# Batch 0's queries in two blocks, the first layer beginning on block one while block two is scored

## Chip, cores, metric

One core of one Trainium2 chip. The metric is the device time of a run in microseconds (us). Every time quoted is a median of runs unless said otherwise.

## The reference

Sigmoid attention over 8 batches of 12 heads, 448 positions and 64 columns a head; then an MLP with a tanh-approximated gelu on 3584 rows.

```python
scores = scale * np.matmul(q, k.transpose(0, 1, 3, 2)) - np.log(S)     # S = 448
attn = 1.0 / (1.0 + np.exp(-scores))
x = heads_side_by_side(np.matmul(attn, v))                             # 3584 x 768
h = x @ w_in                                                           # 768 x 2048
g = 0.5 * h * (1.0 + np.tanh(c * (h + 0.044715 * h * h * h)))
out = g @ w_out                                                        # 2048 x 768
```

## The kernel before

The kernel plans its own order. It holds a list of operations with dependencies and assumed costs, plays them through on paper, and emits each engine's instructions in the order found. Four heads make a group (3 groups a batch); a unit is a group's scores against 64 keys (7 units a group). "qk" is a score matmul, "av" a value matmul, "A" the first layer, "B" the second, "evx" the copy of an attention result into `xT`, the input of A. Heads are scored through the sigmoid function in batch 0, later through tanh and an affine step on the vector engine (DVE), since 1/(1+exp(-x)) is 0.5 tanh(x/2) + 0.5.

```python
units = [(g, j) for g in range(G) for j in range(NJ)]
EARLY = ("v0 q2 v1 v2 q3 v3 w0 w1 q4 v4 w2 q5 v5 w3 o0 o1 o2 o3").split()   # order of the early loads
# ... in make_qk, for unit n of group g: four 64x64 matmuls of 448 columns, then
if g < SIG * NG:                                  # batch 0: sigmoid, on the scalar engine (ACT)
    tanh[n] = aff[n] = plan.add(Op("sig%d" % n, "ACT",
        lambda e: e.activation(at[as_][:], both, AF.Sigmoid, bias=bias, scale=scale),
        [op, old], 2 * S / 1.2 + 60, 2 * S / 1.2 + 210, prio=(1, n)))
    if n == SIG * NG * NJ - 1:                    # after the last sigmoid: touch gelu's table once
        plan.add(Op("warm2", "ACT", lambda e: e.activation(warm[:], warm[:], AF.Gelu_apprx_tanh),
                    [tanh[n]], 1500.0, 1500.0))
else:                                             # later batches: tanh (ACT), then affine (DVE)
    ...
# ... in make_a: A of batch b, column block fc of the 2048, six 128x128 matmuls of 448 columns
deps = [prev] + [evac[(b, kt)] for kt in range(KT)]
# ...
ev = plan.add(Op("gelu%d.%d" % (b, fc), "ACT", ..., gdeps, S / 1.2 + 50, S / 1.2 + 190, prio=(0, b)))
```

The last two numbers of an operation are what the plan believes that it occupies and takes. No plan cost depends on the function computed before it. A has to wait for all three groups of its batch, so in batch 0 it waits for all 21 sigmoids.

Of the kernel before, what the change touches and what calls it, by code (L numbers as in the profile page):

```python
# [266 lines left out]
def bass_sigmoid_attention__then__act_gelu_tanh_kernel(  # L267
# [24 lines left out]
    NQT = 3  # L292
# [12 lines left out]
    with contextlib.ExitStack() as stack:  # L305
# [73 lines left out]


        G = B * NG
        units = [(g, j) for g in range(G) for j in range(NJ)]
        cast_q, cast_k, tr_q, tr_k, ld_q, ld_k, ld_v = {}, {}, {}, {}, {}, {}, {}
        freed_q, freed_k = {}, {}
        qk, tanh, aff, av, evac = {}, {}, {}, {}, {}
        trans = []

        EARLY = ("v0 q2 v1 v2 q3 v3 w0 w1 q4 v4 w2 q5 v5 w3 o0 o1 o2 o3").split()
# [19 lines left out]
        def load_qk(g):  # L408
            b, i = divmod(g, NG)
            s = g % NQF  # L410
            for (nm, src, dst, low, ld, cast, freed) in (("k", k, kf, kb, ld_k, cast_k, freed_k),
                                                         ("q", q, qf, qb, ld_q, cast_q, freed_q)):
                ap = flat4(src, b, i).rearrange("(c p x) -> p c x", c=2, p=128)
                if low_load(nm, g):
# [9 lines left out]
                                    + ([lambda: w_out_ld[3][0]] if PE_TR * NG <= g < PE_TR * NG + NG else []), 500.0, 0.0,  # L424
                                    prio=(2, g), sem="ld%s%d" % (nm, s), pkt=(16, 85.0)))
# [16 lines left out]
        def cast_qk(g):  # L442
            s = g % NQF
            for (nm, src, dst, ld, cast, freed) in (("k", kf, kb, ld_k, cast_k, freed_k),
                                                    ("q", qf, qb, ld_q, cast_q, freed_q)):
                if low_load(nm, g):
# [6 lines left out]
                                      [ld[g]] + later(freed, g - NQF), 660.0, 720.0, prio=(1, g), alts=alts))  # L453
# [16 lines left out]
        def trans_ready(t):  # L470
            if not trans or eye.end is None or eye.end > t or free_pairs(t) < 1:
                return False
            g, nm, src, dst, cast, tr, freed, after = trans[0]
            return g in cast and cast[g].end is not None and cast[g].end <= t
# [35 lines left out]
        def make_qk(n, t):  # L510
            g, j = units[n]
# [5 lines left out]
            both = ps[:, x:y + 1, 0:S]  # L517
            kv, qv = by_half(kT[s], g), by_half(qT[s], g)

            def fn(e):  # L520
                r = None
                for (a, c, half) in ((0, 0, 0), (0, 1, 1), (1, 1, 0), (1, 0, 1)):
                    d = slice(64 * c, 64 * c + 64)
                    r = mm(ps[64 * half:64 * half + 64, (x, y)[a], 0:S],  # L524
                           kv[d, a, j, :], qv[d, a, :, :],
# [3 lines left out]
            qk[(g, j)] = op = Op("qk%d.%d" % (g, j), "PE", fn, [tr_q[g], tr_k[g]] + prev,  # L529
                                 4 * 2.5 + S / 2.4, 165.0, mode=64)  # L530
            pg, pj = units[n - NAT] if n >= NAT else (None, None)
            old = av[pg] if pg is not None else None
            if g < SIG * NG:
                tanh[n] = aff[n] = plan.add(Op("sig%d" % n, "ACT",
                                               lambda e: e.activation(at[as_][:], both, AF.Sigmoid,  # L535
                                                                      bias=bias, scale=scale),
                                               [op, old], 2 * S / 1.2 + 60, 2 * S / 1.2 + 210, prio=(1, n)))
                if n == SIG * NG * NJ - 1:
                    plan.add(Op("warm2", "ACT", lambda e: e.activation(warm[:], warm[:], AF.Gelu_apprx_tanh),
                                [tanh[n]], 1500.0, 1500.0))  # L540
            else:
                tanh[n] = plan.add(Op("tanh%d" % n, "ACT",
                                      lambda e: e.activation(th[ts][:], both, AF.Tanh,  # L543
                                                             bias=0.5 * bias, scale=0.5 * scale),
                                      [op, aff.get(n - NTH)], 2 * S / 1.2 + 60, 2 * S / 1.2 + 210, prio=(1, n)))
                aff[n] = plan.add(Op("aff%d" % n, "DVE",
                                     lambda e: e.tensor_scalar(at[as_][:], th[ts][:], 0.5, 0.5,  # L547
                                                               op0=ALU.mult, op1=ALU.add),
                                     [tanh[n], old], 640.0, 710.0, prio=(2, n)))
# [6 lines left out]
        def make_av(g, t):  # L556
            b, i = divmod(g, NG)
# [4 lines left out]
            for j in range(NJ):  # L562
                n = g * NJ + j
                as_ = n % NAT

                def fn(e, j=j, as_=as_):
                    r = None
                    for (a, c, half) in ((0, 0, 0), (0, 1, 1), (1, 0, 1), (1, 1, 0)):
                        d = slice(64 * half, 64 * half + 64)
                        slot = half if a == 0 else 1 - half  # L570
                        r = mm(ps[64 * c:64 * c + 64, banks[a], 0:S],  # L571
                               vb[s][d, slot, j, :],
                               at[as_][d, a, :],
# [4 lines left out]
                ops.append(Op("av%d.%d" % (g, j), "PE", fn, deps, 4 * 2.5 + S / 2.4, 165.0, mode=64))  # L578
            av_open.append((g, banks, ops))
# [4 lines left out]
        def close_av():  # L584
            g, banks, ops = av_open.pop()
            b, i = divmod(g, NG)
            for j in range(NJ):
                ops[j].deps = [d for d in ops[j].deps + [aff[g * NJ + j]]]
            av[g] = ops[-1]
            xb = b % NXT  # L590
            for a in range(2):
                deps = [ops[-1]]
                if b >= NXT:
                    deps.append(a_last[b - NXT])
                op = plan.add(Op("evx%d.%d" % (g, a), "ANY",
                                 lambda e, who, a=a: copy(e, xT[xb][:, 2 * i + a, :], ps[:, banks[a], 0:S], who),
                                 deps, 0, 0, prio=(0, g),
                                 alts=copy_alts(S) if b else {"DVE": copy_alts(S)["DVE"]}))
# [351 lines left out]
```

## Time and profile before

| | before |
|---|---|
| time (first 3 runs) | 395.24 us |
| span | 393.7 us |
| tensor engine (PE) busy | 378.2 us, 96% |
| first sigmoid, last sigmoid's end | 9.74 us, 27.7 us |
| first A | 29.60 us |
| table loads on ACT | 2 |

The page's busy line, and two lines of its chain of waits:

```profile
PE 378.2 (96%) x3344; PEld 196.0 (50%) x3344; DVE 135.6 (34%) x227; ACT 240.7 (61%) x377; POOL 50.9 (13%) x82
...
PE 92%; ACT 4%; DMA 2%; DVE 0%; issue 0%; SPq 0%; ACTq 0%
```

Busy time says that PE is nearly full, but the matmuls are counted with their modelled ends. I kept a ledger. Its rates come from dense stretches of this trace: 12 matmuls of A (448 columns) take 2.27 us and 16 of B (384 columns) 2.60 us, which makes 2.4 columns per ns and 2.5 ns more for each matmul; 28 transposes take 0.25 us, and the four 64x64 matmuls of a unit count as one pass of their columns. The work so counted is the useful PE time, 356.6 us in all; what remains of the elapsed time is "excess". In the kernel before, excess reaches 19.0 us at 30 us and grows by 14.5 us in the next 320 us. So over half of it lies in the head, and there time is to be had. ACT around its only later table load, with start, duration and instruction:

```profile
26.62 1.09 ACT L535 ACTIVATE at<-ps 128x896 bf16<-128x896 f32 x1
27.42 1.10 ACT L543 ACTIVATE th<-ps 128x896 f32<-128x896 f32 x1
28.54 1.28 ACT L539 ACT_TABLE_LOAD   x1
29.83 0.20 ACT L539 ACTIVATE warm<-warm 128x1 f32<-128x1 f32 x1
```

Two neighbouring starts are 0.80 us apart, though each takes about 1 us: activations overlap. The load doesn't overlap anything. And PE in the same place (the bracket is idle time before it and what ended it):

```profile
26.95 0.38 PE L524 MATMUL ps<-qT,kT 64*64 64x448 bf16 x4 [0.24 <-ACT at L535]
27.16 0.36 PE L571 MATMUL ps<-at,vb 64*64 64x448 bf16 x4
27.76 0.38 PE L524 MATMUL ps<-qT,kT 64*64 64x448 bf16 x4 [0.24 <-ACT at L535]
...
29.60 2.44 PE L616 MATMUL ps<-xT,w_in 128*128 128x448 bf16 x12 [0.38 <-DVE xT L335]
```

In each 0.81 us PE has two units of work, which take 0.19 us each in dense stretches; the trace counts it busy for 0.57 us and idle for 0.24, waiting for a sigmoid.

### The profile page before, as it was taken

The numbers are of one execution on the slowest core, as the hardware profiler recorded it, in microseconds if no ns is written. First come the engines' busy times: TensorE is split into PE (matmuls) and PEld (weight loads), VectorE is DVE, ScalarE is ACT, GpSimd is POOL, SyncE is SP. The second block draws the span as 40 slices with busy tenths as digits, with TensorE's granted clock in tenths as the row PEclk, the third lists the DMA queues.
The fourth block names the chain that finished last, engine by engine and source line by source line (L and its number), as shares of the span: only waits on it lengthen the run. The fifth ranks groups of instructions, "written<-read, shape, count | busy, mean of one in ns | idle before, by whom it ended". The sixth has DMA issues, their size and how long they took to land.

```text
span 393.7 us, 7728 instructions
## 1 busy us (share of the span) xinstructions
PE 378.2 (96%) x3344; PEld 196.0 (50%) x3344; DVE 135.6 (34%) x227; ACT 240.7 (61%) x377; POOL 50.9 (13%) x82
## 2 busy tenths in 40 slices
PE   2879999999999999999999999999999999999996
PEld 1424545555544554554554555555454555555563
DVE  3426643136545515545444343343333210000000
ACT  1999973477779757777657666576647632333211
POOL 6992110011102010101110101101000000000000
PEclk9999999999999999999999999999999999999999
DMA  8999999728689466768767448727211011111133
GB/s 230 199 199 203 210 190 301 163 52 176 166 214 207 123 140 155 162 157 184 179 115 180 133 78 177 183 47 182 65 40 42 2 40 42 40 42 40 40 82 80
DMA packets 63490, 51.76 MB, mean 131 GB/s; under 512 B 36192, under 2 KB 60000, under 8 KB 63456
## 3 DMA queue, kind: packets, MB, share of 16 engines
q1 hardware_dynamic: 48848, 37.53, 37.8%
q0 software_dynamic: 14528, 13.64, 21.9%
q8 instruction: 26, 0.43, 0.4%
q10 hardware_dynamic: 80, 0.10, 0.1%
q14 instruction: 8, 0.07, 0.1%
HBM read 45.61 MB, written 11.01 MB: 144 GB/s over the span
## 4 chain that ended last, share of the span: by engine, by line
PE 92%; ACT 4%; DMA 2%; DVE 0%; issue 0%; SPq 0%; ACTq 0%
PE ps L616 37%; PE ps L653 37%; PE ps L524 9%; PE ps L571 8%; ACT at L535 3%; DMA kf<-in_k_dram 2%; ACT th L543 1%; PE ps L490 1%; DVE xT L335 0%; ACT gT L629 0%; SPq L422 0%; DVE kb L335 0%; ACT xT L334 0%; ACT ob L334 0%; ACTq L888 0%
## 5 line engine op out<-in xcount | busy, mean ns | idle before, releaser
L616 PE MATMUL ps<-xT,w_in 128*128 128x448 bf16 x768 | 155.5, 353 | 0.5 <-DVE xT L335 0.4
L653 PE MATMUL ps<-w_out,gT 128*128 128x384 bf16 x896 | 153.1, 326 | 0.0
L547 DVE TENSOR_SCALAR at<-th 128x896 bf16<-128x896 f32 x147 | 92.0, 626 | 139.0 <-ACT th L543 138.8
L543 ACT ACTIVATE th<-ps 128x896 f32<-128x896 f32 x147 | 129.1, 929 | 0.1
L653 PEld LDWEIGHTS ps<-w_out,gT 128*128 128x128 bf16 x896 | 86.3, 98 | 63.3 <-ACT th L543 2.9
L616 PEld LDWEIGHTS ps<-xT,w_in 128*128 128x128 bf16 x768 | 71.7, 98 | 76.7 <-ACT th L543 3.9
L629 ACT ACTIVATE gT<-ps 128x448 bf16<-128x448 f32 x128 | 71.2, 556 | 43.2 <-PE ps L616 43.1
L334 ACT ACTIVATE ob<-ps 128x384 f32<-128x384 f32 x56 | 27.5, 490 | 95.4 <-PE ps L653 95.4
L524 PE MATMUL ps<-qT,kT 64*64 64x448 bf16 x672 | 48.8, 368 | 4.0 <-ACT at L535 3.7
L436 POOL DMA_DIRECT2D vb<-in_v_dram x24 | 14.5, 604 | 216.8 <-PE ps L524 213.9
L571 PE MATMUL ps<-at,vb 64*64 64x448 bf16 x672 | 40.1, 356 | 0.2
L524 PEld LDWEIGHTS ps<-qT,kT 64*64 64x64 bf16 x672 | 15.0, 106 | 32.3 <-issue 14.4
L571 PEld LDWEIGHTS ps<-at,vb 64*64 64x64 bf16 x672 | 19.9, 109 | 11.8 <-issue 1.3
L535 ACT ACTIVATE at<-ps 128x896 bf16<-128x896 f32 x21 | 17.4, 971 | 8.0 <-PE ps L524 7.9
L335 DVE CAST xT<-ps 128x448 bf16<-128x448 f32 x27 | 16.4, 618 | 11.5 <-PE ps L571 11.5
L335 DVE CAST kb<-kf 128x896 bf16<-128x896 f32 x20 | 12.5, 624 | 18.1 <-DMA kf<-in_k_dram 17.8
L438 POOL DMA_DIRECT2D vb<-in_v_dram x24 | 17.6, 733 | 0.2 <-issue 0.2
L335 DVE CAST qb<-qf 128x896 bf16<-128x896 f32 x20 | 12.7, 634 | 6.7 <-DMA qf<-in_q_dram 6.6
L334 ACT ACTIVATE xT<-ps 128x448 bf16<-128x448 f32 x21 | 11.9, 566 | 2.6 <-PE ps L571 2.6
L708 POOL DMA_DIRECT2D w_in<-in_moe_w_in_dram x16 | 9.9, 655 | 0.0
L490 PE MATMUL ps<-ident,kb 64*64 64x64 bf16 x168 | 3.0, 217 | 5.9 <-DVE kb L335 5.9
L490 PEld LDWEIGHTS ps<-ident,kb 64*64 64x64 bf16 x168 | 2.5, 129 | 7.1 <-issue 5.6
(18 smaller groups left out, 26.0 us busy)
## 6 DMA issues: line engine op xcount, KB each, us to landing
out_dram<-ob SPq DMA_DIRECT2D x54, 192.0 KB, 2.7
kf<-in_k_dram SPq DMA_DIRECT2D x20, 448.0 KB, 4.8
qf<-in_q_dram SPq DMA_DIRECT2D x20, 448.0 KB, 6.0
vb<-in_v_dram POOLq DMA_DIRECT2D x48, 112.0 KB, 5.7
w_in<-in_moe_w_in_dram POOLq DMA_DIRECT2D x16, 192.0 KB, 11.3
w_out<-in_moe_w_out_dram POOLq DMA_DIRECT2D x4, 768.0 KB, 23.6
kb<-in_k_dram POOLq DMA_DIRECT2D x4, 224.0 KB, 9.0
qb<-in_q_dram POOLq DMA_DIRECT2D x4, 224.0 KB, 9.5
```

The source lines that it names most:

```text
L334: return e.activation(o, i, AF.Copy)
L335: return e.tensor_copy(o, i)
L436: a = plan.add(Op("ldv%da" % g, "SWQ", lambda e, d=dst[0:64], ap=lo: e.dma_start(d, ap), deps, 610.0, 0.0, prio=order_v(g), sem="ldv%da" % ...
L438: c = plan.add(Op("ldv%db" % g, "SWQ", lambda e, d=dst[64:128], ap=hi: e.dma_start(d, ap), deps, 610.0, 0.0, prio=order_v(g), sem="ldv%db" ...
L524: r = mm(ps[64 * half:64 * half + 64, (x, y)[a], 0:S], kv[d, a, j, :], qv[d, a, :, :], start=True, stop=True)
L535: lambda e: e.activation(at[as_][:], both, AF.Sigmoid, bias=bias, scale=scale),
L543: lambda e: e.activation(th[ts][:], both, AF.Tanh, bias=0.5 * bias, scale=0.5 * scale),
L547: lambda e: e.tensor_scalar(at[as_][:], th[ts][:], 0.5, 0.5, op0=ALU.mult, op1=ALU.add),
L571: r = mm(ps[64 * c:64 * c + 64, banks[a], 0:S], vb[s][d, slot, j, :], at[as_][d, a, :], start=(j == 0), stop=(j == NJ - 1))
L616: r = mm(ps[:, bank, 0:S], w_in[:, kt, fc * 128:(fc + 1) * 128], xT[xb][:, kt, :], start=(kt == 0), stop=(kt == KT - 1))
L629: lambda e: e.activation(gT[:, fc, col:col + S], ps[:, bank, 0:S], AF.Gelu_apprx_tanh),
L653: r = mm(ps[:, bank, 0:EH], gT[:, fc, col:col + 128], w_out[:, fc, half * EH:(half + 1) * EH], start=(fc == 0), stop=(fc == FC - 1))
```

## The change

Batch 0's queries are cut at column 256. All units of block one are scored first, their values multiplied, and A may begin on 256 columns while block two's 192 columns are scored. To serve this, the weights of A are loaded ahead of group 3, k1's cast waits until q0 is transposed, two more pairs of transposed buffers are there, and batch 2's first loads wait for batch 1's last one rather than for the last piece of `w_out`. The core of the diff (cut; the rest carries the block's bounds through, raises the plan's cost of a load from 85 to 89 ns a packet, and lets a transpose wait for what it follows):

```diff
-    NQT = 3
+    NQT = 5
+    CUT = 256
...
+        def parts(b):
+            return ((0, CUT), (CUT, S)) if b == 0 else ((0, S),)
-        units = [(g, j) for g in range(G) for j in range(NJ)]
+        for b in range(B):
+            for lo, hi in parts(b):
+                for g in range(b * NG, b * NG + NG):
+                    jobs.append((g, lo, hi, [len(units) + j for j in range(NJ)]))
+                    units += [(g, j, lo, hi, len(jobs) - 1) for j in range(NJ)]
...
-        EARLY = ("v0 q2 v1 v2 q3 v3 w0 w1 q4 v4 w2 q5 v5 w3 o0 o1 o2 o3").split()
+        EARLY = ("v0 q2 v1 v2 w0 w1 w2 w3 q3 v3 o0 o1 o2 o3 q4 v4 q5 v5").split()
...
-   + ([lambda: w_out_ld[3][0]] if PE_TR * NG <= g < PE_TR * NG + NG else [])
+   + ([lambda: ld_q[2 * NG - 1]] if PE_TR * NG <= g < PE_TR * NG + NG else [])
...
-   [ld[g]] + later(freed, g - NQF)
+   [ld[g]] + later(freed, g - NQF) + (later(tr_q, 0) if g == 1 else [])
...
-            deps = [prev] + [evac[(b, kt)] for kt in range(KT)]
+            deps = [prev] + [evac[(b, kt, lo)] for kt in range(KT)]
```

More of the change, by code (lines that the diff above doesn't have):

```diff
@@ L378, in give @@
             bank_busy[i] = False
+        def parts(b):
+            return ((0, CUT), (CUT, S)) if b == 0 else ((0, S),)
         G = B * NG
-        units = [(g, j) for g in range(G) for j in range(NJ)]
+        units = []
+        jobs = []
+        for b in range(B):
[3 more added lines that the diff above has]
+                    units += [(g, j, lo, hi, len(jobs) - 1) for j in range(NJ)]
+        sig_last = max(n for n in range(len(units)) if units[n][0] < SIG * NG)
+        before = [0.0]
+        for u in units:
+            before.append(before[-1] + (u[3] - u[2]) / (S * NG * NJ))
         cast_q, cast_k, tr_q, tr_k, ld_q, ld_k, ld_v = {}, {}, {}, {}, {}, {}, {}
         freed_q, freed_k = {}, {}
-        qk, tanh, aff, av, evac = {}, {}, {}, {}, {}
+        qk, tanh, aff, av, av_done, evac = {}, {}, {}, {}, {}, {}
         trans = []
-        EARLY = ("v0 q2 v1 v2 q3 v3 w0 w1 q4 v4 w2 q5 v5 w3 o0 o1 o2 o3").split()
+        EARLY = ("v0 q2 v1 v2 w0 w1 w2 w3 q3 v3 o0 o1 o2 o3 q4 v4 q5 v5").split()
         def order_q(g):
@@ L423, in load_qk @@
                                     later(cast, g - NQF) + later(qk, g - NQT, NJ - 1)
-                                    + ([lambda: w_out_ld[3][0]] if PE_TR * NG <= g < PE_TR * NG + NG else []), 500.0, 0.0,
-                                    prio=(2, g), sem="ld%s%d" % (nm, s), pkt=(16, 85.0)))
+                                    + ([lambda: ld_q[2 * NG - 1]] if PE_TR * NG <= g < PE_TR * NG + NG else []), 500.0, 0.0,
+                                    prio=(2, g), sem="ld%s%d" % (nm, s), pkt=(16, 89.0)))
         def load_v(g):
@@ L452, in cast_qk @@
                                       lambda e, who, o=o_ap, i=i_ap: copy(e, o, i, who),
-                                      [ld[g]] + later(freed, g - NQF), 660.0, 720.0, prio=(1, g), alts=alts))
+                                      [ld[g]] + later(freed, g - NQF) + (later(tr_q, 0) if g == 1 else []), 660.0, 720.0, prio=(1, g), alts=alts))
         def transpose_qk(g):
@@ L473, in trans_ready @@
             g, nm, src, dst, cast, tr, freed, after = trans[0]
+            if any(d() is None for d in after):
+                return False
             return g in cast and cast[g].end is not None and cast[g].end <= t
@@ L510, in make_qk @@
         def make_qk(n, t):
-            g, j = units[n]
+            g, j, lo, hi, job = units[n]
+            w = hi - lo
             s = g % NQT
@@ L516, in make_qk @@
             prev = [bank_free[x], bank_free[y]]
-            both = ps[:, x:y + 1, 0:S]
+            both = ps[:, x:y + 1, 0:w]
             kv, qv = by_half(kT[s], g), by_half(qT[s], g)
@@ L523, in fn @@
                     d = slice(64 * c, 64 * c + 64)
-                    r = mm(ps[64 * half:64 * half + 64, (x, y)[a], 0:S],
-                           kv[d, a, j, :], qv[d, a, :, :],
+                    r = mm(ps[64 * half:64 * half + 64, (x, y)[a], 0:w],
+                           kv[d, a, j, :], qv[d, a, lo // 64:hi // 64, :],
                            start=True, stop=True)
                 return r
-            qk[(g, j)] = op = Op("qk%d.%d" % (g, j), "PE", fn, [tr_q[g], tr_k[g]] + prev,
-                                 4 * 2.5 + S / 2.4, 165.0, mode=64)
-            pg, pj = units[n - NAT] if n >= NAT else (None, None)
-            old = av[pg] if pg is not None else None
+            op = Op("qk%d.%d" % (g, j), "PE", fn, [tr_q[g], tr_k[g]] + prev,
+                                 4 * 2.5 + w / 2.4, 165.0, mode=64)
+            if hi == S:
+                qk[(g, j)] = op
+            old = av_done[units[n - NAT][4]] if n >= NAT else None
             if g < SIG * NG:
                 tanh[n] = aff[n] = plan.add(Op("sig%d" % n, "ACT",
-                                               lambda e: e.activation(at[as_][:], both, AF.Sigmoid,
+                                               lambda e: e.activation(at[as_][:, :, 0:w], both, AF.Sigmoid,
                                                                       bias=bias, scale=scale),
-                                               [op, old], 2 * S / 1.2 + 60, 2 * S / 1.2 + 210, prio=(1, n)))
-                if n == SIG * NG * NJ - 1:
+                                               [op, old], 2 * w / 1.2 + 60, 2 * w / 1.2 + 210, prio=(1, n)))
+                if n == sig_last:
                     plan.add(Op("warm2", "ACT", lambda e: e.activation(warm[:], warm[:], AF.Gelu_apprx_tanh),
@@ L542, in make_qk @@
                 tanh[n] = plan.add(Op("tanh%d" % n, "ACT",
-                                      lambda e: e.activation(th[ts][:], both, AF.Tanh,
+                                      lambda e: e.activation(th[ts][:, :, 0:w], both, AF.Tanh,
                                                              bias=0.5 * bias, scale=0.5 * scale),
-                                      [op, aff.get(n - NTH)], 2 * S / 1.2 + 60, 2 * S / 1.2 + 210, prio=(1, n)))
+                                      [op, aff.get(n - NTH)], 2 * w / 1.2 + 60, 2 * w / 1.2 + 210, prio=(1, n)))
                 aff[n] = plan.add(Op("aff%d" % n, "DVE",
-                                     lambda e: e.tensor_scalar(at[as_][:], th[ts][:], 0.5, 0.5,
+                                     lambda e: e.tensor_scalar(at[as_][:, :, 0:w], th[ts][:, :, 0:w], 0.5, 0.5,
                                                                op0=ALU.mult, op1=ALU.add),
-                                     [tanh[n], old], 640.0, 710.0, prio=(2, n)))
+                                     [tanh[n], old], w / 0.7, w / 0.7 + 70, prio=(2, n)))
             give(x, tanh[n])
@@ L554, in bass_sigmoid_attention__then__act_gelu_tanh_kernel, with make_av @@
         a_last = {}
-        def make_av(g, t):
-            b, i = divmod(g, NG)
+        def make_av(job, t):
+            g, lo, hi, ns = jobs[job]
+            w = hi - lo
             s = g % NVB
@@ L562, in make_av @@
             for j in range(NJ):
-                n = g * NJ + j
+                n = ns[j]
                 as_ = n % NAT
@@ L570, in fn @@
                         slot = half if a == 0 else 1 - half
-                        r = mm(ps[64 * c:64 * c + 64, banks[a], 0:S],
+                        r = mm(ps[64 * c:64 * c + 64, banks[a], 0:w],
                                vb[s][d, slot, j, :],
-                               at[as_][d, a, :],
+                               at[as_][d, a, 0:w],
                                start=(j == 0), stop=(j == NJ - 1))
@@ L577, in make_av @@
                 deps = [aff.get(n)] + (list(ld_v[g]) + prev if j == 0 else [])
-                ops.append(Op("av%d.%d" % (g, j), "PE", fn, deps, 4 * 2.5 + S / 2.4, 165.0, mode=64))
-            av_open.append((g, banks, ops))
+                ops.append(Op("av%d.%d" % (g, j), "PE", fn, deps, 4 * 2.5 + w / 2.4, 165.0, mode=64))
+            av_open.append((job, banks, ops))
             return ops
@@ L584, in close_av @@
         def close_av():
-            g, banks, ops = av_open.pop()
+            job, banks, ops = av_open.pop()
+            g, lo, hi, ns = jobs[job]
+            w = hi - lo
             b, i = divmod(g, NG)
             for j in range(NJ):
-                ops[j].deps = [d for d in ops[j].deps + [aff[g * NJ + j]]]
-            av[g] = ops[-1]
+                ops[j].deps = [d for d in ops[j].deps + [aff[ns[j]]]]
+            av_done[job] = ops[-1]
+            if hi == S:
+                av[g] = ops[-1]
             xb = b % NXT
@@ L595, in close_av @@
                 op = plan.add(Op("evx%d.%d" % (g, a), "ANY",
-                                 lambda e, who, a=a: copy(e, xT[xb][:, 2 * i + a, :], ps[:, banks[a], 0:S], who),
+                                 lambda e, who, a=a: copy(
+                                     e, xT[xb][:, 2 * i + a, lo:hi], ps[:, banks[a], 0:w], who),
                                  deps, 0, 0, prio=(0, g),
-                                 alts=copy_alts(S) if b else {"DVE": copy_alts(S)["DVE"]}))
+                                 alts=copy_alts(w) if b else {"DVE": copy_alts(w)["DVE"]}))
                 give(banks[a], op)
-                evac[(b, 2 * i + a)] = op
+                evac[(b, 2 * i + a, lo)] = op
         w_in_ld = {}
@@ L606, in bass_sigmoid_attention__then__act_gelu_tanh_kernel, with make_a @@
         b_last = {}
-        def make_a(b, fc, t):
+        a_todo = [(b, fc, lo, hi) for b in range(B) for lo, hi in parts(b) for fc in range(FC)]
+        a_end = {b: max(x for x in range(len(a_todo)) if a_todo[x][0] == b) for b in range(B)}
+        a_before = [0.0]
+        for x in a_todo:
+            a_before.append(a_before[-1] + (x[3] - x[2]) / (S * FC))
+        def make_a(b, fc, lo, hi, t):
             bank = take(t)
             xb = b % NXT
+            w = hi - lo
             prev = bank_free[bank]
@@ L615, in fn @@
                 for kt in range(KT):
-                    r = mm(ps[:, bank, 0:S], w_in[:, kt, fc * 128:(fc + 1) * 128], xT[xb][:, kt, :],
+                    r = mm(ps[:, bank, 0:w], w_in[:, kt, fc * 128:(fc + 1) * 128], xT[xb][:, kt, lo:hi],
                            start=(kt == 0), stop=(kt == KT - 1))
                 return r
-            deps = [prev] + [evac[(b, kt)] for kt in range(KT)]
+            deps = [prev] + [evac[(b, kt, lo)] for kt in range(KT)]
             if b == 0:
                 deps += w_in_ld[fc * 128 // WSL]
-            op = Op("a%d.%d" % (b, fc), "PE", fn, deps, KT * (S / 2.4 + 2.5), 165.0, mode=128)
+            op = Op("a%d.%d" % (b, fc), "PE", fn, deps, KT * (w / 2.4 + 2.5), 165.0, mode=128)
             col = (b % 2) * S
@@ L628, in make_a @@
             ev = plan.add(Op("gelu%d.%d" % (b, fc), "ACT",
-                             lambda e: e.activation(gT[:, fc, col:col + S], ps[:, bank, 0:S],
+                             lambda e: e.activation(gT[:, fc, col + lo:col + hi], ps[:, bank, 0:w],
                                                     AF.Gelu_apprx_tanh),
-                             gdeps, S / 1.2 + 50, S / 1.2 + 190, prio=(0, b)))
+                             gdeps, w / 1.2 + 50, w / 1.2 + 190, prio=(0, b)))
             give(bank, ev)
-            gelu[(b, fc)] = ev
+            gelu.setdefault((b, fc), []).append(ev)
             a_last[b] = op
@@ L656, in fn @@
                 return r
-            deps = [prev] + [gelu[(b, fc)] for b in {x[0] for x in two} for fc in range(FC)]
+            deps = [prev] + [x for b in {x[0] for x in two} for fc in range(FC) for x in gelu[(b, fc)]]
             if t_ < 8:
@@ L717, in load_w_out @@
                                        after, 760.0, 0.0, prio=prio, sem="wo%d" % n, pkt=(32, 117.0)))]
-        state = {"n": 0, "av": 0, "queue": [], "a": (0, 0), "b": 0, "h": 0, "avj": 0, "loaded": 0}
+        state = {"n": 0, "av": 0, "queue": [], "a": 0, "b": 0, "h": 0, "avj": 0, "loaded": 0}
         def load(g):
@@ L730, in a_ready @@
         def a_ready(t):
-            b, fc = state["a"]
-            if b >= B or any((b, kt) not in evac for kt in range(KT)):
-                return False
-            if b >= 2 and (b - 2) not in b_done:
+            if state["a"] >= len(a_todo):
+                return False
+            b, fc, lo, hi = a_todo[state["a"]]
+            if any((b, kt, lo) not in evac for kt in range(KT)) or b >= 2 and (b - 2) not in b_done:
                 return False
-            deps = [evac[(b, kt)] for kt in range(KT)]
+            deps = [evac[(b, kt, lo)] for kt in range(KT)]
             if b == 0:
@@ L746, in b_ready @@
             for b in {x[0] for x in two}:
-                if (b, FC - 1) not in gelu:
+                if state["a"] <= a_end[b]:
                     return False
-                deps.append(gelu[(b, FC - 1)])
+                deps += gelu[(b, FC - 1)]
             for x in w_out_ld.values():
@@ L756, in qk_ready, with units_done @@
                 return False
-            g, j = units[n]
-            if g not in tr_q or n >= NAT and units[n - NAT][0] not in av:
+            g = units[n][0]
+            if g not in tr_q or n >= NAT and units[n - NAT][4] not in av_done:
                 return False
             return all(d.end is not None and d.end <= t for d in (tr_q[g], tr_k[g]))
-        def units_done(g, t):
+        def units_done(job, t):
             n = 0
             while state["avj"] + n < NJ:
-                d = aff.get(g * NJ + state["avj"] + n)
+                d = aff.get(jobs[job][3][state["avj"] + n])
                 if d is None or d.end is None or d.end > t:
@@ L772, in av_begins @@
         def av_begins(t):
-            g = state["av"]
-            if g >= G:
+            if state["av"] >= len(jobs):
                 return False
@@ L777, in av_begins @@
                 return True
+            g = jobs[state["av"]][0]
             b = g // NG
-            if b >= NXT and ((b - NXT) not in a_last or state["a"][0] <= b - NXT):
+            if b >= NXT and state["a"] <= a_end[b - NXT]:
                 return False
-            return all(d.end is not None and d.end <= t for d in ld_v.get(g, (zero,))) and g in ld_v \
-                and free_banks(t) >= 2
+            return all(d.end is not None and d.end <= t for d in ld_v[g]) and free_banks(t) >= 2
         def av_take(m, t):
-            g = state["av"]
             if not av_open:
-                make_av(g, t)
+                make_av(state["av"], t)
             ops = av_open[-1][2][state["avj"]:state["avj"] + m]
@@ L794, in av_take @@
             return ops
-        UB = NG * NJ
-        LEAD = 2 * UB
+        LEAD = 2.0
+        N2 = next(n for n in range(len(units)) if units[n][0] == 2 * NG)
         def pe_next(pl, t):
@@ L803, in pe_next @@
             n = state["n"]
-            a_prog = state["a"][0] + state["a"][1] / FC
+            a_prog = a_before[state["a"]]
             b_prog = (state["b"] + 0.5 * state["h"]) * 2 / NJ
@@ L816, in pe_next @@
             can = 0
-            if n <= LEAD + UB * 0.5 * (a_prog + b_prog):
+            if before[n] <= LEAD + 0.5 * (a_prog + b_prog):
                 while can < BURST and qk_ready(t, n + can):
@@ L820, in pe_next @@
             left = sum(1 for x in range(max(0, n - 4), n) if tanh[x].end is None or tanh[x].end > t)
-            hungry = n < 2 * UB and left <= 1
+            hungry = n < N2 and left <= 1
             m = units_done(state["av"], t) if av_begins(t) else 0
@@ L843, in pe_next @@
                 return ops[0]
-            if whole and (n == len(units) or state["av"] < 2 * NG and not can):
+            if whole and (n == len(units) or state["av"] < len(jobs) and jobs[state["av"]][0] < 2 * NG and not can):
                 ops = av_take(m, t)
@@ L850, in pe_next @@
             if go_a:
-                b, fc = state["a"]
-                op = make_a(b, fc, t)
-                state["a"] = (b, fc + 1) if fc + 1 < FC else (b + 1, 0)
+                op = make_a(*a_todo[state["a"]], t)
+                state["a"] += 1
                 return op
@@ L873, in bass_sigmoid_attention__then__act_gelu_tanh_kernel @@
         plan.run()
-        assert state["n"] == len(units) and state["av"] == G and state["b"] == NT, state
+        assert state["n"] == len(units) and state["av"] == len(jobs) and state["b"] == NT, state
         waits, level = emit(plan, None, None)
```

## The prediction

> **What bounds it now.** The page's busy table puts the tensor engine at 378.2 us of a 393.7 us span. Dense stretches of its timeline give 1.135 us for a first-layer column block (six 448-wide matmuls), 2.60 us for sixteen second-layer matmuls, 0.19 us for a score or value unit; times the counts, about 357 us of work. The chain of waits runs through it except at the head, where from 9.7 to 27.8 us it runs through the scalar engine: 21 sigmoids of 896 columns, one every 0.81 us. The first first-layer matmul starts at 29.60 us, after about 10 us of matmul work. The rest is some 0.12 us at each change between 64- and 128-row matmuls and a 3.4 us tail.
>
> **Intent.** The sigmoids of block one take, by the slope between 448 (0.42 us apart) and 896 columns (0.80), about 0.475 us each. With q0's cast ahead of k1's, scoring starts about 1 us earlier (8.7 us), so block one is scored at about 19 us and the first layer could start 9 us sooner, worth some 5 to 9 us.
>
> **What it also does.** Gelu of block one now alternates with sigmoid of block two on the scalar engine. The instruction listing of the changed kernel shows what the kernel's own schedule does not count: 20 activation-table loads instead of 2; 18 new ones stand before the last sigmoid. A load took 1.283 us in the trace (28.54 us). The Trainium skill, "ScalarE: Activation LUTs", section "What ACT_TABLE_LOAD costs", gives the same 1283 ns, and a drain that makes 2.66 us of it; in this trace the tanh before it started at 27.42 and the next activation at 29.83, 1.6 us beyond the 0.80 us slot, so I take 1.5 us.
>
> Scalar time to the last sigmoid: 8.7 + 0.3 (group 2's load) + 21 x 0.475 + 21 x 0.366 + 10 gelus x 0.26 + 18 x 1.5 = 56 us. The eight accumulator banks don't let the tensor engine run ahead, so nearly all of this is critical. By then the tensor engine has done only 16.4 us of its work (42 half scores, 11 narrow first-layer blocks, 8 transposes); before, about 33 us at 54.8 us.
>
> Sum: 56 + 340 us of work left + 122 mode changes x 0.12 + 3.4 tail + about 2.5 us of stalls (gelu backlog; the values of groups 4 and 5 waiting for scores just issued before the first layer of batch 1) = 416.5 us span, plus 1.6 us between span and time: **418 us**, range 412 to 427. Faster by over 2%: 2%; within 2%: 4%; slower by over 2%: 94%.
>
> **What the profile would show.** 20 table loads, 25.7 us; scalar engine near 100% busy from 9 to 55 us; the chain of waits through sigmoid, loads and gelu there; a cycle of 3.6 to 4 us for one first-layer block and two score units; first first-layer matmul near 20 us (this part of the intent works); last sigmoid at 53 to 59 us; from there a dense tensor engine, some 360 us to the end. Weights arrive early enough not to matter.
>
> **What would make it wrong.** Loads that overlap other waits, or a cheaper drain: 412. A switch of 2.66 us, as the skill states: up to 435. The tensor engine's clock dropping in the gaps, or 192-wide matmuls held up by their weight loads (96 x some 20 ns): a few us more. If the listed table loads were not what runs, the gain of 5 to 9 us would show.

## More of the kernel before

Stretches of the run (start:end, length, busy us of PE, PEld, DVE, ACT and POOL with their instructions in brackets, granted PE clock, DMA share, GB/s):

```profile
16.00:24.00 8.00, 6.02 (x140) 2.41 (x136) 3.56 (x6) 8.00 (x11) 8.00 (x14) 1.00 1.23 196
24.00:32.00 8.00, 6.19 (x96) 2.26 (x88) 3.30 (x6) 7.97 (x11) 6.51 (x10) 1.00 1.25 203
32.00:40.00 8.00, 8.00 (x99) 3.55 (x102) 4.69 (x8) 7.92 (x13) 1.56 (x2) 1.00 1.25 204
40.00:48.00 8.00, 7.78 (x146) 4.15 (x146) 5.29 (x10) 7.21 (x12) 1.30 (x2) 1.00 1.16 210
48.00:56.00 8.00, 8.00 (x88) 3.54 (x80) 4.27 (x7) 6.76 (x11) 1.20 (x2) 1.00 1.17 208
```

## The result

| | before | after |
|---|---|---|
| time | 395.09 us (394.68 to 395.37) | 424.19 us (423.55 to 424.44) |
| ratio | | 1.0729 (1.0707 to 1.0751) |
| span | 393.7 us | 421.8 us |
| table loads | 2 | 20 |
| first A | 29.60 us | 24.01 us |
| last sigmoid's end | 27.7 us | 59.16 us |

A ratio is the mean time of one kernel's runs over the mean of the other's in the same rounds, so it isn't quite the ratio of the medians. Executions over 1.5% slower than the fastest of the same kernel are left out of the means. Brackets are the lowest and the highest of four runs for times, and 95% intervals for ratios.

The same lines of the page after:

```profile
PE 392.2 (93%) x3608; PEld 209.7 (50%) x3608; DVE 137.2 (33%) x235; ACT 268.2 (64%) x430; POOL 48.6 (12%) x82
...
PE 85%; ACT 11%; DMA 2%; DVE 1%; issue 1%; SPq 0%
...
L661 ACT ACT_TABLE_LOAD x9 | 11.5, 1283 | 0.1
L554 ACT ACT_TABLE_LOAD x9 | 11.5, 1283 | 0.1
```

ACT's share of the chain rose from 4% to 11%, and the two groups of table loads are 18 times 1.283 us. The stretches:

```profile
16.00:24.00 8.00, 7.04 (x131) 2.53 (x123) 2.27 (x6) 7.96 (x17) 8.00 (x13) 0.84 1.21 192
24.00:32.00 8.00, 3.42 (x38) 2.05 (x42) 0.00 (x0) 7.89 (x11) 5.15 (x8) 0.80 1.24 203
32.00:40.00 8.00, 5.20 (x54) 2.79 (x51) 0.62 (x2) 7.91 (x11) 1.21 (x2) 0.50 1.18 209
40.00:48.00 8.00, 4.15 (x48) 2.47 (x50) 0.00 (x0) 7.92 (x11) 0.00 (x0) 0.50 1.16 210
48.00:56.00 8.00, 6.93 (x55) 3.62 (x48) 0.62 (x2) 7.90 (x12) 1.19 (x2) 0.50 1.24 199
```

From 24 to 56 us ACT is busy over 98% (7.89 to 7.92 of 8 us), and PE, which was nearly full from 32 us on before, is not. The number after POOL's is the granted PE clock: it falls to 0.50. One period of ACT there:

```profile
34.81 0.87 ACT L554 ACTIVATE at<-ps 128x384 bf16<-128x384 f32 x2
35.70 1.28 ACT L661 ACT_TABLE_LOAD   x1
37.00 0.38 ACT L661 ACTIVATE gT<-ps 128x256 bf16<-128x256 f32 x1
37.39 1.28 ACT L554 ACT_TABLE_LOAD   x1
38.68 0.87 ACT L554 ACTIVATE at<-ps 128x384 bf16<-128x384 f32 x2
```

Two block-two sigmoids, a load, one gelu, a load: 3.87 us from 34.81 to 38.68, of which 2.57 are loads. PE's side of it:

```profile
39.22 0.54 PE L542 MATMUL ps<-qT,kT 64*64 64x192 bf16 x8 [1.55 <-ACT at L554]
39.69 1.46 PE L648 MATMUL ps<-xT,w_in 128*128 128x256 bf16 x6
43.08 0.54 PE L542 MATMUL ps<-qT,kT 64*64 64x192 bf16 x8 [1.93 <-ACT at L554]
...
60.20 1.46 PE L648 MATMUL ps<-xT,w_in 128*128 128x256 bf16 x6
61.59 1.33 PE L542 MATMUL ps<-qT,kT 64*64 64x448 bf16 x12
62.86 2.18 PE L648 MATMUL ps<-xT,w_in 128*128 128x256 bf16 x18
```

It waits 1.55 and 1.93 us for sigmoids. With eight accumulator banks it can't run ahead of ACT by more than a few units.

### The profile page after: what moved, and what is told of

It is laid out like the page before. It is cut to its first block, busy times and chain, and to the rows that moved or that the text cites. A ratio compares the mean times of both kernels' runs of the same rounds, so it can differ in the third digit from the quotient of the medians.

```text
span 421.8 us, 8325 instructions
## 1 busy us (share of the span) xinstructions
PE 392.2 (93%) x3608; PEld 209.7 (50%) x3608; DVE 137.2 (33%) x235; ACT 268.2 (64%) x430; POOL 48.6 (12%) x82
## 4 chain that ended last, share of the span: by engine, by line
PE 85%; ACT 11%; DMA 2%; DVE 1%; issue 1%; SPq 0%
PE ps L685 35%; PE ps L648 34%; PE ps L542 9%; PE ps L591 7%; ACT at L554 4%; ACT L554 3%; ACT L661 3%; DMA qf<-in_q_dram 2%; ACT gT L661 1%; DVE xT L336 0%; PE ps L507 0%; SPq L437 0%; DVE at L566 0%; DVE qb L336 0%; ACT ob L335 0%
## 5 line engine op out<-in xcount | busy, mean ns | idle before, releaser
L648 PE MATMUL ps<-xT,w_in 128*128 128x448 bf16 (+2 forms) x864 | 162.5, 341 | 1.4 <-ACT gT L661 0.9
L648 PEld LDWEIGHTS ps<-xT,w_in 128*128 128x128 bf16 x864 | 80.9, 100 | 76.0 <-ACT gT L661 5.6
L661 ACT ACTIVATE gT<-ps 128x448 bf16<-128x448 f32 (+2 forms) x144 | 73.3, 515 | 40.0 <-PE ps L648 39.9
L542 PE MATMUL ps<-qT,kT 64*64 64x448 bf16 (+2 forms) x756 | 53.9, 358 | 14.8 <-ACT at L554 11.7
L591 PE MATMUL ps<-at,vb 64*64 64x448 bf16 (+2 forms) x756 | 43.0, 346 | 2.1 <-ACT at L554 1.1
L542 PEld LDWEIGHTS ps<-qT,kT 64*64 64x64 bf16 x756 | 17.8, 110 | 45.8 <-ACT at L554 20.5
L451 POOL DMA_DIRECT2D vb<-in_v_dram x24 | 14.6, 606 | 221.6 <-PE ps L591 203.2
L336 DVE CAST xT<-ps 128x448 bf16<-128x448 f32 (+2 forms) x35 | 18.2, 539 | 39.7 <-PE ps L591 39.6
L591 PEld LDWEIGHTS ps<-at,vb 64*64 64x64 bf16 x756 | 22.9, 114 | 13.4 <-DVE at L566 1.7
L554 ACT ACTIVATE at<-ps 128x512 bf16<-128x512 f32 (+1 forms) x42 | 20.5, 542 | 9.3 <-PE ps L542 9.1
L453 POOL DMA_DIRECT2D vb<-in_v_dram x24 | 15.3, 639 | 0.2 <-issue 0.2
L661 ACT ACT_TABLE_LOAD x9 | 11.5, 1283 | 0.1
L554 ACT ACT_TABLE_LOAD x9 | 11.5, 1283 | 0.1
## 6 DMA issues: line engine op xcount, KB each, us to landing
w_out<-in_moe_w_out_dram POOLq DMA_DIRECT2D x4, 768.0 KB, 20.6
```

What stands on the lines that cost most here:

```text
L336: return e.tensor_copy(o, i)
L451: a = plan.add(Op("ldv%da" % g, "SWQ", lambda e, d=dst[0:64], ap=lo: e.dma_start(d, ap), deps, 610.0, 0.0, prio=order_v(g), sem="ldv%da" % ...
L453: c = plan.add(Op("ldv%db" % g, "SWQ", lambda e, d=dst[64:128], ap=hi: e.dma_start(d, ap), deps, 610.0, 0.0, prio=order_v(g), sem="ldv%db" ...
L542: r = mm(ps[64 * half:64 * half + 64, (x, y)[a], 0:w], kv[d, a, j, :], qv[d, a, lo // 64:hi // 64, :], start=True, stop=True)
L554: lambda e: e.activation(at[as_][:, :, 0:w], both, AF.Sigmoid, bias=bias, scale=scale),
L591: r = mm(ps[64 * c:64 * c + 64, banks[a], 0:w], vb[s][d, slot, j, :], at[as_][d, a, 0:w], start=(j == 0), stop=(j == NJ - 1))
```

## The experiments

Theory at the start: the loss is the table loads, and the split without them gains nothing either. Rival A: without the loads the split gains the 5 to 9 us of the prediction. Rival B: the narrow blocks or the new order of loads cost most.

Twelve kernels in three rounds. Each was also run against the kernel before on the same chip, whose medians in the three rounds were 395.42, 395.65 and 394.99 us.

### The change without its added table loads

```diff
-    AF.Gelu_apprx_tanh
+    AF.Sigmoid if b == 0 and lo == 0 and fc < 10 else AF.Gelu_apprx_tanh
```

I compared the instruction lists of all engines with those of the changed kernel: apart from the function and the 18 loads they are the same.

> The changed kernel, instruction for instruction, but the ten gelus that stand between sigmoids are computed as sigmoids (a wrong result, on purpose), so that 18 of its 20 table loads are gone. Theory (the loads are the whole loss and a bit more): the last sigmoid ends near 33.5 us instead of 59.2, the granted clock stays at 1.00, and the span is 33.5 + 361 = 394.5 us, so 395 to 398 us of time: the split by itself gains nothing, since the 25 more mode changes and the stalls eat it. Rival A (as my prediction has it, the earlier first layer is worth 5 to 9 us without the loads): 386 to 390 us. Rival B (the split or the new order of loads is what costs most): over 405 us.

Measured: 399.75 us (ratio 1.0113, 1.0097 to 1.0129), wrong result as meant. The same stretch of ACT:

```profile
28.84 0.87 ACT L554 ACTIVATE at<-ps 128x384 bf16<-128x384 f32 x2
29.60 0.38 ACT L661 ACTIVATE gT<-ps 128x256 bf16<-128x256 f32 x1
29.89 0.87 ACT L554 ACTIVATE at<-ps 128x384 bf16<-128x384 f32 x2
```

The period is 1.05 us. The last sigmoid ends at 35.88 us instead of 59.16, 23.3 us sooner, and the time falls by 424.19 - 399.75 = 24.4 us. PE's clock shows too; the same two instructions as above:

```profile
38.12 0.83 PE L648 MATMUL ps<-xT,w_in 128*128 128x256 bf16 x6
38.88 0.76 PE L542 MATMUL ps<-qT,kT 64*64 64x448 bf16 x12
39.57 2.14 PE L648 MATMUL ps<-xT,w_in 128*128 128x256 bf16 x18
```

A narrow A and three units occupy 39.57 - 38.12 = 1.45 us here; after the change 62.86 - 60.20 = 2.66 us, at half clock, 1.2 us more. This can't simply be added to the 23.3 us: from the last sigmoid to the end the profiled execution took 362.5 us without the loads and 362.6 with them, and the two spans differ by 421.8 - 398.4 = 23.4 us. So the sum does not show the clock's 1.2 us, and the last 1 us of the 24.4 is the difference between medians and profiled executions. So some 24 of the 29.1 us are settled: they come from the loads, nearly all of them before the last sigmoid. Rival A, my own claim that the split alone brings 5 to 9 us, is refuted: without the loads the kernel is still 4.3 us slower than before. Rival B is refuted too, but my theory's figure was 2 us low.

### Half of the loads

```diff
-    AF.Gelu_apprx_tanh
+    AF.Sigmoid if b == 0 and lo == 0 and fc < 5 else AF.Gelu_apprx_tanh
```

> The changed kernel with the first five of the ten interleaved gelus computed as sigmoids (a wrong result, on purpose): 10 of the 18 additional table loads are gone, 8 stay. Theory (the price is per load): 424.2 - 24.4 x 10/18 = 410.6, 409 to 413 us. Rival (the first few loads, or the fall of the tensor engine's clock that they bring, make most of the loss): outside 406 to 415 us.

Measured: 410.72 us (1.0387, 1.0351 to 1.0424), wrong result as meant. The first ten loads taken away save (424.19 - 410.72)/10 = 1.35 us each, the other eight (410.72 - 399.75)/8 = 1.37. The price is per load.

### The same price in the other kernel

```diff
-    e.activation(at[as_][:], both, AF.Sigmoid,            # kernel before
+    e.activation(at[as_][:], both, AF.Gelu_apprx_tanh if n % 2 else AF.Sigmoid,
```

> The kernel before, where every second of its 21 sigmoids is computed as gelu (a wrong result, on purpose): 20 table loads more in the head, no split. Theory (a switch costs its 1.283 us and a drain of some 0.1 to 0.2 us, and all of it shows in the time while the scalar engine bounds the head): 395.3 + 20 x 1.43 = 424, 422 to 426 us. Rival (a switch costs 2.66 us): 448 us. Rival (loads are partly hidden by waits for the tensor engine): under 418 us.

Measured: 425.91 us (1.0766), wrong result as meant; (425.91 - 395.65)/20 = 1.51 us a load. In the trace an activation and a load take 2.22 us together (22.25 to 24.47):

```profile
22.25 1.28 ACT L535 ACT_TABLE_LOAD   x1
23.54 0.92 ACT L535 ACTIVATE at<-ps 128x896 bf16<-128x896 f32 x1
24.47 1.28 ACT L535 ACT_TABLE_LOAD   x1
```

That is 1.41 us more than the 0.81 us between sigmoids before: 1.28 for the load and 0.13 for the lost overlap. The last sigmoid ends at 55.66 us, 27.95 us later than before, 1.40 us a load. Most of the rest comes just after it, where 12 matmuls of A, 2.44 us in the kernel before, run at about half that rate:

```profile
57.94 4.49 PE L616 MATMUL ps<-xT,w_in 128*128 128x448 bf16 x12 [0.46 <-DVE xT L335]
```

A switch of 2.66 us is not seen.

### A right result with one table load

Sigmoid only for block one; block two through tanh, which is in gelu's table set.

```diff
-            if g < SIG * NG:
+            if g < SIG * NG and lo == 0:
```

> The changed kernel with a right result and one table load in the middle: block two's scores go through tanh (in gelu's table set) and the affine step on the vector engine; only block one uses sigmoid. Theory: 395 to 399 us, 2 table loads in all, last tanh of block two near 36 us. Rival A: 387 to 391. Rival B: over 405 us.

Measured: 400.89 us (1.0149, 1.0127 to 1.0172), correct, but above the 395 to 399 us expected. The loads are mended, and the split still loses 5.5 us. The next runs ask to what.

### All edits but the split

```diff
-            return ((0, CUT), (CUT, S)) if b == 0 else ((0, S),)
+            return ((0, S),)
```

> All edits of the change except the split: batch 0 is one block again, the order of the weight loads, the five transposed buffers and the earlier cast of q0 stay. Theory: 393 to 396 us, first first-layer matmul near 29 us, 2 table loads. If the new order of loads were to blame (rival B): over 400 us.

Measured: 398.9 us (1.0093, 1.0075 to 1.0111), between the two expectations. The kernel without the split is as slow, within 1 us, as the split without its loads (399.75, in the same rounds); the split with a right result (400.89) is 2.0 us slower than it. So the split as such gains nothing and may cost up to 2 us, and 3.5 us are lost without it, by the small edits around it. Every edit makes the plan lay out the program anew, so such parts need not add up.

### The split, but the first layer held until the last sigmoid

```diff
             b, fc, lo, hi = a_todo[state["a"]]
+            if sig_last not in tanh or tanh[sig_last].end is None or tanh[sig_last].end > t:
+                return False
```

> The split stays, but the first layer may not begin before the last sigmoid is done: 42 narrow sigmoids, then one table load, then all gelus. Theory: last sigmoid near 31 us, span 396, time 396 to 400 us: the split costs 1 to 4 us for nothing, the interleaving of two table sets costs the other 25. Rival B (the split costs most): over 405 us.

Measured: 401.01 us (1.015, 1.0118 to 1.0183), correct. The last sigmoid ended at 32.87 us rather than 31, the first A followed at 33.23 us, and the time is 1 us above the 396 to 400 us expected. Starting A at 23.75 us, as the version with a right result does (400.89 us), or after the last sigmoid makes no difference that these runs show.

### Only the new order of loads

```diff
-        EARLY = ("v0 q2 v1 v2 q3 v3 w0 w1 q4 v4 w2 q5 v5 w3 o0 o1 o2 o3").split()     # kernel before
+        EARLY = ("v0 q2 v1 v2 w0 w1 w2 w3 q3 v3 o0 o1 o2 o3 q4 v4 q5 v5").split()
```

> The kernel before with one line changed: the new order of the early loads (all of the first layer's weights ahead of group 3, all of the second layer's ahead of groups 4 and 5). No split, nothing else. The last runs left 4 us that the table loads don't explain, and the kernel without the split had 3.5 of them. Theory: the load order is their cause: 398 to 399 us, groups 3 to 5 are scored later, so the second layer begins earlier (near 55 us instead of 64), batch 1's first layer later, with a wait of about 1 us before it. Rival (the earlier cast of q0, the five buffers or the other load condition): 395 to 396 us.

Measured: 400.89 us (1.0139, 1.0103 to 1.0175): one line costs 5.2 us, 2 us more than expected. Its first A on PE:

```profile
28.26 0.38 PE L571 MATMUL ps<-at,vb 64*64 64x448 bf16 x4 [0.43 <-ACT at L535]
29.91 8.78 PE L616 MATMUL ps<-xT,w_in 128*128 128x448 bf16 x30 [1.27 <-DVE xT L335]
```

Group 3 isn't there yet (its keys land at 31.9 us, before at 16.3), so PE has nothing to do beside the last sigmoids (before, it had group 3's transposes and first scores), waits 1.27 us, and its clock falls (0.82 granted from 24 to 32 us and 0.76 from 32 to 40, against 1.00 before): these 30 matmuls take 8.78 us, where 12 took 2.44 us in the kernel before, so 6.1 at that rate. The ledger says the same: excess is 20.6 us at 30 us and 23.8 at 40, against 19.0 and 19.7 before; of the final difference of 5.7 us in span 4.1 are there at 40 us. The second layer begins at 56.2 us instead of 64.1, as expected; the wait before batch 1's A is only 0.39 us.

### Only the other edits, with the old order of loads

The kernel of "all edits but the split", with the old EARLY line put back.

> The complement: the changed kernel without the split and with the old order of loads, so only the earlier cast of q0, the five transposed buffers and the changed load condition are left. Theory (the load order costs the 3.5 us): 395 to 396.5 us. Rival: 398 to 399 us.

Measured: 400.17 us (1.0118, 1.0099 to 1.0138). It lies above both expectations, and my theory falls: the load order isn't the only cause. The trace points to the load condition, though no run has this condition alone. The first loads of batch 2 start at 36.80 us, not at 57.98, because with the old order batch 1's last load comes early; the weights are still on their way. DVE then stands at a cast of batch 2, and ACT and PE behind it:

```profile
44.22 0.63 DVE L336 CAST kb<-kf 128x896 bf16<-128x896 f32 x1 [1.66 <-DMA kf<-in_k_dram]
...
48.41 0.63 DVE L336 CAST qb<-qf 128x896 bf16<-128x896 f32 x1 [2.50 <-DMA qf<-in_q_dram]
49.68 0.92 ACT L562 ACTIVATE th<-ps 128x896 f32<-128x896 f32 x1 [1.61 <-DVE at L566]
50.65 1.31 PE L648 MATMUL ps<-xT,w_in 128*128 128x448 bf16 x6 [2.04 <-ACT th L562]
```

DVE stands idle for 2.50 us, ACT then waits 1.61 us for the affine step behind that cast, and PE 2.04 us for the tanh after it. So the new load order and the other edits belong together: the order alone costs 5.2 us, the others without it 4.5, and all of them 3.5 us. That it is the load condition among the others is read from this trace and not tested.

### Only the earlier cast

```diff
-    [ld[g]] + later(freed, g - NQF), 660.0, 720.0            # kernel before
+    [ld[g]] + later(freed, g - NQF) + (later(tr_q, 0) if g == 1 else []), 660.0, 720.0
```

> The kernel before with one line changed: k1's cast waits until q0 has been transposed, so that scoring starts sooner; nothing else. Theory (the run of all the small edits with the old load order was slow because its loads of batch 2 start 21 us earlier and collide, not because of the cast): 394 to 397 us, first sigmoid near 9.0 instead of 9.74. Rival (the cast is what costs): 399 us or more.

Measured: 396.62 us (1.0033, 1.0014 to 1.0053). The first sigmoid starts at 8.99 us, 0.75 us sooner, and nothing is won by it; the time is over 1 us longer:

```profile
8.99 1.73 ACT L535 ACTIVATE at<-ps 128x896 bf16<-128x896 f32 x2 [6.76 <-PE ps L524]
12.08 3.35 ACT L535 ACTIVATE at<-ps 128x896 bf16<-128x896 f32 x4 [1.37 <-PE ps L524]
15.62 12.26 ACT L535 ACTIVATE at<-ps 128x896 bf16<-128x896 f32 x15 [0.20 <-PE ps L524]
27.60 1.09 ACT L543 ACTIVATE th<-ps 128x896 f32<-128x896 f32 x1
```

ACT waits 1.37 us at 12.08, and the first tanh starts at 27.60, against 27.42 before.

### Another cut

Block two by tanh as above, and `CUT = 320`.

> The right version without the loads (block two by tanh), cut at 320 instead of 256 columns, so the first layer starts later but has wider matmuls. Theory (the split gains nothing, whatever the cut, because the scalar engine's work in the head is the same and the later stalls come from the order of loads): 399 to 402 us, like the cut at 256 (400.9). If the narrow matmuls and the number of mode changes were what costs: 397 or less.

Measured: 399.04 us (1.0103, 1.0074 to 1.0132), correct; at the lower edge of what was expected. It may be a little better than the cut at 256 (1.0149, other rounds); it doesn't reach the kernel before.

### Another order of loads

```diff
+        EARLY = ("v0 q2 v1 v2 w0 q3 v3 w1 w2 q4 v4 w3 q5 v5 o0 o1 o2 o3").split()
+    CUT = 192                                                # and block two by tanh
```

> An attempt to beat both: block two by tanh, cut at 192, and an order of loads between the old and the new one (group 3 after the first quarter of the first layer's weights, group 4 after three quarters, second layer's weights last), so that batch 1 is scored in time. If the lateness of batch 1 is what the split kernel still loses: 394 to 397 us. If any departure from the order that the kernel before was tuned with costs: 399 to 402 us.

Measured: 403.85 us (1.0212, 1.0182 to 1.0241), outside both expectations. A begins at 23.17 us with four blocks, but the next A comes only at 30.85 us, and the ledger's excess is 25.2 us at 40 us against 19.7 before. No version of mine beats the kernel before.

### A gap that waits for nothing

The split kernels show a gap of 0.6 to 2 us on PE in the middle of a unit, for which the profile names no cause. After the change:

```profile
13.10 0.73 PE L542 MATMUL ps<-qT,kT 64*64 64x256 bf16 x5
15.29 0.42 PE L542 MATMUL ps<-qT,kT 64*64 64x256 bf16 x3 [1.46 <-issue]
```

Counting from the start, 221 matmuls stand before it, in each of these kernels (the first line holds the 217th to the 221st). One more kernel does q0's transposes twice (block two by tanh):

```diff
-                for j in range(NJ):
+                for j in list(range(NJ)) * (2 if (g, nm) == (0, "q") else 1):
```

> The version with block two by tanh, and q0's transposes done twice (28 more matmuls early on, same result). It asks about the gap of 0.6 to 2 us that all four split kernels show in the middle of a score unit, always after 221 matmuls, with nothing waited for. If the gap belongs to a place in the instruction stream (a block of instructions that arrives late): it is again after about 221 matmuls, now amid q2's transposes, 28 matmuls earlier in the work. Rival (it belongs to that score unit or its data): after 249 matmuls, in the same unit.

Measured once, state unknown: 401.06 us, correct. The gap:

```profile
13.09 0.31 PE L507 MATMUL ps<-ident,qb 64*64 64x64 bf16 x5
14.57 0.53 PE L507 MATMUL ps<-ident,qb 64*64 64x64 bf16 x23 [1.17 <-issue]
```

Again 221 matmuls stand before it, though they are 28 less of the work: it is now five matmuls into q2's transposes. In the eight split kernels whose traces I looked at, this count is the same, while the gap begins at times from 13.4 to 15.0 us. So it belongs to a place in the instruction stream, not to that unit. The Trainium skill, "Runtime: NRT & Kernel Launch", section "Instruction fetch mechanics", says that instructions come by DMA in blocks of 256 and that this is mostly hidden. A block that comes late fits: the DMA share is at 1.2 there, and the gap ends between 14.57 and 15.69 us in all eight. The kernel before gets to that matmul at about 15.8 us and shows no gap. The fetch itself is not seen in these traces, so this stays an inference. If it is right, narrow matmuls are dearer in the head, since they use up instructions faster; no run tests that.

## Why the prediction was right

**The step that decided it.** The kernel's plan doesn't know the table loads. The instruction listing does, and 18 loads were taken at 1.5 us each, nearly all on the critical path: 27 us. Measured in the time: 24.4 us, or 1.36 us each. In ACT's own period it is half of 3.87 - 1.05, so 1.41 us each; the term was right in kind and a little high.

**The last sigmoid** was put at 56 us (53 to 59) and ended at 59.16. The sum gave 0.3 us to waits for group 2; ACT waited 0.87 us at 11.39 and 1.71 us at 15.76, the latter behind the gap just described. This term was mis-sized by 2.3 us.

**Where luck helped.** Without its 27 us for the loads, the sum puts the last sigmoid at 29 us; the run without the loads ended it at 35.88, 6.9 us later, and the loads moved it by 23.3 us and not by 27. So 3.7 us too much for the loads hid part of what was missing in the rest of the head. The range held for the right main reason, but the total came as near as it did because two errors have opposite signs.

**From there to the end** 360.5 us were expected and 362.6 came. The halved clock, which the text had among the risks and not in the sum, costs 1.2 us just after the last sigmoid; but the run without the loads, at full clock, also took 362.5 us, so the clock doesn't explain the difference of 2.1 us. The stall before batch 1's A, put with others at 2.5 us, is visible at 98 to 102 us in waits of 0.85, 0.16 and 0.45 us.

**What was wrong: "worth some 5 to 9 us" without the loads.** A did start 5.6 us sooner (24.01 us, not near 20 as predicted), so that step of the intent works in part. But the step from "A starts sooner" to "time is won" fails: up to there ACT bounds the head (without the loads it is busy for 7.87 of the 8 us from 16 to 24), and the same score columns have to pass through it in any order. Columns that A gains at 24 us are columns not scored yet. By the ledger, the split without loads has done 11.1 us of useful PE work at 30 us, the kernel before 11.0; at 40 us it is 1.6 us behind, at 80 us 4.3. By then it has paid for more mode changes (143 against 117 in all, from the instruction lists; at the prediction's 0.12 us each the 26 are about 3 us, an estimate) and for the surrounding edits. How much is due to which is not shown: the kernel without the split has only 123 mode changes and loses 3.5 us, the one with the layer held 125 and loses 5.6. The earlier cast, counted as 1 us, gave none.

**"Weights arrive early enough not to matter"** was right for the weights and missed what their place in the queue does to group 3: this order of loads alone costs the kernel before 5 us.

What stays open: the exact shares of the remaining 4.3 us. The load order and the cast each cost something alone, and not in a way that adds up; the load condition, the two more pairs of buffers and the plan's changed cost of a load were not run alone. Every edit gives another plan with other stalls.

## What to carry to other kernels

Before two activation functions are interleaved, count the table loads in the compiled listing, and put their price into any plan of one's own; here each cost 1.35 to 1.51 us of the kernel's time. Starting a consumer earlier gained nothing here while the engine that feeds the whole stage was the limit: ask how much useful work is done at a later common time, not when the consumer starts. A tuned order of loads is a part of the schedule: moving weights ahead of the next group's data cost the kernel before 5.2 us, more than the 4.3 us that the change lost beside its table loads.

## What the Trainium skill lacked or had wrong

- "ScalarE: Activation LUTs", section "What ACT_TABLE_LOAD costs": 1283 ns agrees (1.28 us in every trace here). The drain of about 1380 ns, 2.66 us in all, doesn't: 20 loads cost 1.51 us each in time, and a load and its lost overlap 1.41 us in the trace (1.40 us each up to the last sigmoid's end).
- The same page, section "Table sets: the hidden batching unit": that sigmoid's set holds tanh agrees with the trace (no load between the last sigmoid and the tanh at 27.42 us). It doesn't say that gelu_apprx_tanh's set holds tanh as well; here gelus and tanhs alternate from 31 us on with no load, which is what makes the mended version possible.
- "TensorE: Matmul & The Clock Gate", section "Why this matters for your kernels": the advice to avoid idle gaps of over about 3 us is not enough by itself; the same page, section "A second HAM failure mode: psum-queue depth-cycling", does tell of a clock that switches back and forth when PE idles briefly but often. Here, from 16 us on, the longest gap of PE after the change was 2.47 us, and the clock was at 0.50 from 32 to 56 us; with gaps of at most 1.27 us, on the other order of loads, the first 30 matmuls of A took 8.78 us instead of about 6.1.
- "Runtime: NRT & Kernel Launch", section "Instruction fetch mechanics": it calls the cost of a block boundary mostly hidden. A gap of 0.6 to 2 us after 221 matmuls, bound to the place in the instruction stream, looks like one that isn't, with the DMA share at 1.2.
